# Two pairs of attention units to a visit of the tensor engine: all scores together, all values together

## The chip, the cores and the metric

The kernel runs on one core of one Trainium2 chip. A core has a matrix engine (TensorE, PE in the profile, with its weight loads as PEld), a vector engine (VectorE, DVE), a scalar engine (ScalarE, ACT), a general engine (GpSimd, POOL) and a sync engine (SyncE, SP) that here issues DMAs. Each engine runs its own instructions in the order in which the program lists them, and they wait for each other with semaphores. Matrix products are written to PSUM, which has eight banks; the other data lie in SBUF. The metric is the device time of one execution in microseconds (us).

## The reference

Banded attention over 8 batches, 8 heads, 576 positions and head size 64, followed by a feed-forward layer. Everything is float32.

```python
scores = scale * np.matmul(q, k.transpose(0, 1, 3, 2))
mask = (rel >= 0) & (rel < 64)            # rel = query position - key position
scores = np.where(mask, scores, -1e9)
attn = softmax(scores)                     # exp(s - max), divided by (sum + 1e-9)
x = np.matmul(attn, v)                     # 8*576 = 4608 tokens of 8*64 = 512 columns
h = x @ w_in                               # 512 -> 2048
out = np.maximum(0.01 * h, h) @ w_out      # 2048 -> 512
```

## The kernel before

**Units and pairs.** The attention is cut into 72 units: 64 queries of one batch with all 8 heads. A unit sees 128 keys, its own block of 64 and the one before. Two units make a pair `m` (36 of them), and a pair is one step of the attention. The feed-forward layer is cut into 9 chunks of 512 tokens, four pairs each, and each chunk into 16 steps, one for each block of 128 of the 2048 hidden columns.

**Feed-forward.** In a step, `mm1(c, f)` (line 450) makes one block of h from x with 12 matmuls of 128x128 by 128x512: x and the weights are split into a high and a low part, and three products are summed over four blocks of 128. ScalarE then applies the leaky maximum and casts the result to its high part `gh` (lines 462 and 468), VectorE subtracts to get the low part `gl` (line 472). `mm2` (line 488) multiplies `gh` and `gl` with the second weights into four accumulator banks, `o0` to `o3`, with 12 more matmuls (line 504). `mm2` of a step is issued after `mm1` of the next, so that the scalar and vector work of a step lies beside matmuls. When a chunk is done, `evict` (line 510) copies the four banks out on ScalarE into two buffers and stores them; `flush` calls it.

**Attention of one pair.** From pair 8 on it goes so:

- `scores_2(u)` (line 361): 64 matmuls of 64x64 by 64x64 (line 234, in `quarter_scores`), into two PSUM banks. Scores lie with keys across partitions. It also issues the loads of the next k and q on SyncE's queue.
- `shield_2(u)` (line 370): VectorE scales and masks both halves of the scores out of PSUM (line 380), GpSimd takes the maximum over the partitions of each half (line 388), VectorE subtracts it (line 393) and ScalarE takes the exponential (line 394). The subtraction of the second half is `second_2(u)`, issued a step later.
- `sums_2(u)` (line 401): GpSimd sums each half over the partitions (line 406).
- `values_2(u)` (line 409): 32 matmuls of 128x64 by 128x64 (line 419) into one bank, and the load of the next v.
- `invert_2(u)` (line 426): VectorE adds 1e-9 to both halves of the sums and takes the reciprocal (lines 431 to 433).
- `norm_2(u)` (line 435): VectorE multiplies the values with it (line 440), ScalarE casts the product to the high part of x (line 443), VectorE subtracts to get the low part (line 444). The next chunk's `mm1` reads both.

The probabilities of a pair lie in one buffer, `probs_of`, so the values of a pair have to be taken before the next pair's scores are shielded.

**Order of the work.** There are three parts: a beginning whose order is written out by hand (`ORDER`, line 45), 16 jobs that finish chunks 0 and 1 (line 581), and the last loop over chunks 2 to 8 (lines 606 to 625). In the last loop a pair takes four steps. In the second of the four, between `mm1` and `mm2`, TensorE does the values of a pair and then the scores of the next; this is called a visit below. In the third step come the second subtraction, the norm and the sums. Lines 628 to 637 tie every engine to the program's order.

PSUM's eight banks are the four accumulators `o0` to `o3`, and `o`, `h`, `s`, `t`. `mm1` takes `o` and `h` in turn (`of_h`), values take `s` or `t` (`of_a`), scores one of either set.

Of the kernel before, what the change touches and what calls it, by code (L numbers as in the profile page):

```python
# [13 lines left out]
F32 = mybir.dt.float32  # L14
F32R = mybir.dt.float32r
U32 = mybir.dt.uint32
AF = mybir.ActivationFunctionType
ALU = mybir.AluOpType
# [3 lines left out]
B, H, S, D = 8, 8, 576, 64  # L22
DM, DF = 512, 2048
NT = B * S
P = 128
NP = H // 2
QB = 64
NQB = S // QB
NU = B * NQB
CH = 512  # L30
NCHUNK = NT // CH
UPC = CH // QB
UNITS = 2
TURNED = 2 * UPC
PACE = 12
ROOMS = 3
OWN = 4
# [37 lines left out]
SCALE = 1.0 / math.sqrt(D)  # L75
# [7 lines left out]
def flat(t):  # L83
    return t.rearrange("p a b -> p (a b)") if len(t.shape) == 3 else t


@with_exitstack
def band_attention_ffn(ctx: ExitStack, tc: tile.TileContext, qT, kB, vW, w_in, w_out, eye_mask, out):
    nc = tc.nc
    const = ctx.enter_context(tc.tile_pool(name="const", bufs=1))  # L90
    ld = ctx.enter_context(tc.tile_pool(name="ld", bufs=2))
# [1 line left out]
    wk = ctx.enter_context(tc.tile_pool(name="wk", bufs=2))  # L93
# [4 lines left out]
    def bank(tag, name):  # L98
        return ps_e.tile([P, 512], F32, tag=tag, name=name)


    of_h, of_a = cycle("oh"), cycle("st")
# [21 lines left out]
        return more[:, m - 2] if m in (2, 3) else qs[m % 2]  # L124

    def k_of(m):
        return more[:, m] if m in (2, 3) else ks[m % 2]

    def v_of(m):
        return vs[m % 2 if m < TURNED // 2 else 0]  # L130

    def v_heads(m, w):
        return v_of(m)[:, w, : H * (D + 1)].rearrange("p (h d) -> p h d", h=H)

    def load_q(m):
        if m < NU // 2:
            nc.sync.dma_start(q_of(m), qT[m])

    def load_k(m):
        if m < NU // 2:  # L140
            nc.sync.dma_start(k_of(m), kB[m])

    def load_v(m):
        if m < NU // 2:
            nc.sync.dma_start(v_of(m)[:, :, : H * (D + 1)], vW[m])

    def key_blocks(u):

# [63 lines left out]
    probs = {}  # L212

    def x_of(u):
        c, w = divmod(u, UPC)
        if c not in xs:
            xs[c] = [xp.tile([P, KT, CH], F32R, tag=f"x{i}", name=f"x{i}_{c}") for i in range(2)]
        return [x[:, :, w * QB : (w + UNITS) * QB] for x in xs[c]]
# [5 lines left out]
    def quarter_scores(m, ps, begun, more=False):  # L224

        q = q_of(m)
        for w in range(UNITS):
            k = key_blocks(UNITS * m + w)
            for p in range(NP):
                for i in range(2):  # L230
                    for j in range(2):
                        s, t = slice(64 * j, 64 * j + 64), slice(64 * i, 64 * i + 64)
                        c = (2 * p + w) * QB
                        nc.tensor.matmul(  # L234
                            ps[j][t, c : c + QB], k[i][s, p], q[s, w, p],
                            start=not begun and (not more or (w, p) == (0, 0)),
                            stop=not begun and not more or (w, p) == (UNITS - 1, NP - 1),
                        )

    def mask_of(u):  # L240

        kinds = [v % NQB == 0 for v in (u, u + 1)]
        if any(kinds):
            return away[:, 1:] if kinds[0] else away[:, :2]
        return away[:, :1]
# [115 lines left out]
    def scores_2(u):  # L361
        if u >= NU:
            return
        ps = [bank(next(t), f"s{u}_{j}") for j, t in enumerate((of_a, of_h))]
        quarter_scores(u // 2, ps, False)
        probs[u] = ps
        load_k(u // 2 + 1)
        load_q(u // 2 + 2)

    def shield_2(u):  # L370

        if u >= NU:
            return
        ps = probs.pop(u)
        a = mask_of(u).bitcast(F32)
        n = a.shape[1]
        a = flat(a)[:, None, :].broadcast_to([P, H // n, n * QB])
        for j in range(2):
            e, s = (x.rearrange("a (b c) -> a b c", c=n * QB) for x in (probs_of[:, j], ps[j]))
            nc.vector.scalar_tensor_tensor(e, s, SCALE, a, ALU.mult, ALU.add)  # L380
            if j == 0:
                first_most = most(u, j)
        exps_2(0, first_most)
        probs[u] = most(u, 1)
# [11 lines left out]
    def second_2(u):  # L396

        if u < NU:
            exps_2(1, probs.pop(u))

    def sums_2(u):
        if u >= NU:
            return
        raw = flat(wk.tile([P, 512, 2], U32, tag="raw", bufs=3, name=f"n{u}")).bitcast(F32)
        for j in range(2):
            nc.gpsimd.partition_all_reduce(raw[:, 512 * j : 512 * j + 512], probs_of[:, j], P, ReduceOp.add)  # L406
        probs[u] = raw

    def values_2(u):
        if u >= NU:  # L410
            return
        raw = probs.pop(u)
        v = [v_heads(u // 2, w) for w in range(2)]
        ps = bank(next(of_a), f"o{u}")
        for w in range(2):
            for p in range(NP):
                for j in range(2):
                    c = (2 * p + w) * QB
                    nc.tensor.matmul(  # L419
                        ps[64 * j : 64 * j + 64, c : c + QB], v[w][:, 2 * p + j, :D], probs_of[:, j, c : c + QB],  # L420
                        start=True, stop=True,
                    )
        probs[u, 0] = ps, raw
        load_v(u // 2 + 1)

    def invert_2(u):
        if u >= NU:
            return
        ps, raw = probs[u, 0]
        r, t = raw[:, :512], raw[:, 512:]  # L430
        nc.vector.tensor_scalar_add(r[:64], r[:64], 1e-9)
        nc.vector.tensor_scalar_add(r[64:], t[64:], 1e-9)
        nc.vector.reciprocal(r, r)  # L433

    def norm_2(u):
        if u >= NU:
            return
        ps, raw = probs.pop((u, 0))
        r, t = raw[:, :512], raw[:, 512:]
        nc.vector.tensor_tensor(t, ps, r, ALU.mult)  # L440
        hi, lo = x_of(u)
        t = t.rearrange("a (b c) -> a b c", b=NP)
        nc.scalar.copy(hi, t)  # L443
        nc.vector.tensor_tensor(lo, t, hi.bitcast(F32), ALU.subtract)  # L444

    g = {}

    def mm1(c, f, part):  # L450
# [37 lines left out]
    def mm2(c, f, part):  # L488


        gh, gl = g.pop((c, f, part.start))
        wh, wl = wo[f]
        for i in range(part.start // P, part.stop // P):
            split = c == 1 or c == 0 and i < 2
            begin = f == 0 or split and f == half
            end = f == FT - 1 or split and f == half - 1
            if begin:
                pool, tag = (ps_o, f"o{i}")
                if c == 1 and f == 0 and i > 1:
                    pool, tag = ps_e, "st"[i - 2]  # L500
                acc[c, i] = pool.tile([P, DM], F32, tag=tag, name=f"acc{c}_{i}_{f}")
            ts = slice(i * P, (i + 1) * P)
            for n, (a, b) in enumerate(((gh, wh), (gh, wl), (gl, wh))):
                nc.tensor.matmul(  # L504
                    acc[c, i], a[:, ts], b, start=begin and n == 0, stop=end and n == 2
                )
            if end:
                due.append(partial(evict, c, i, f, split))
# [24 lines left out]
    def flush():  # L533
        while due:
            due.pop(0)()
# [42 lines left out]
    prev = jobs[-1]  # L578
    jobs = [(c, half + k, whole) for c in range(2) for k in range(half)]
    first_late = len(jobs) - UPC - 3  # L580
    for n, job in enumerate(jobs):
        weave(mm1(*job), late[n * PACE : (n + 1) * PACE])
        if first_late <= n < len(jobs) - 1:
            u = TURNED - 2 + (n - first_late) // 2 * 2
            if (n - first_late) % 2 == 0:
                if u >= TURNED:
                    values_2(u)
                scores_2(u + 2)
                shield_2(u + 2)
            else:  # L590
                second_2(u + 2)
                if u >= TURNED:
                    norm_2(u)
                sums_2(u + 2)
        mm2(*prev)
        flush()
        if first_late < n < len(jobs) - 1 and (n - first_late) % 2 == 0:
            invert_2(u)
        if n == 4:
            reload(0)  # L600
        if n == 14:
            reload(1)
        prev = job


    steps = [(c, f) for c in range(2, NCHUNK) for f in range(FT)]
    for n, (c, f) in enumerate(steps):
        u = 3 * UPC + n // 4 * 2
        for step in mm1(c, f, whole):
            step()  # L610
        if n % 4 == 1:
            values_2(u)
            scores_2(u + 2)
            shield_2(u + 2)
        if n % 4 == 2:
            second_2(u + 2)
            norm_2(u)
            sums_2(u + 2)
        mm2(*prev)
        flush()  # L620
        if n % 4 == 1:
            invert_2(u)
        prev = (c, f, whole)
    mm2(*prev)
    flush()


    last = {}
# [53 lines left out]
```

## Time and profile before

| what | value |
| --- | --- |
| median of 3 runs | 905.27 us (904.88 to 905.3) |
| profiled execution | 906.58 us, of which the span from first to last instruction is 904.8 us |
| VectorE busy | 497.2 us (55%) |
| ScalarE busy | 304.9 us (34%) |
| GpSimd busy | 321.2 us (36%) |
| data read and written in DRAM | 56.62 and 11.01 MB, 75 GB/s over the span |

The profile is that of one execution, and its rows are read so. A row of a timeline has the start in us from the first instruction, the duration, the engine, the line of the kernel, the operation, what it writes and reads, its shape, and how many instructions are merged in it. Matmuls overlap, so the distance between two starts says more than a duration. A row of groups ends with the busy time in us, the mean of one in ns, and the idle time of the engine before them with what ended it.

### The profile page before, as it was taken

The page shows a single profiled execution, that of the slowest core. Times are in us where ns is not written, and L with a number is a line of the kernel's source. Part 1 is how long each engine was busy: PE and PEld are TensorE (multiplying, and loading weights), DVE is VectorE, ACT ScalarE, POOL GpSimd, SP SyncE. Part 2 cuts the span into 40 slices and gives each one's busy share as a digit, 9 for nine tenths or more (in the row PEclk, how much of TensorE's full clock was granted, in tenths as well). Part 3 has the DMA queues.
Part 4 walks back from the last instruction along what each step waited for, and adds up shares of the span by engine and source line. Part 5 has one row for each costly group of instructions (what it writes and reads, how often), then busy time and mean ns, then how long its engine had stood idle before and what let it go on. Part 6 is the DMA issues. An engine that isn't in the chain of part 4 may idle for free.

```text
span 904.8 us, 16195 instructions
## 1 busy us (share of the span) xinstructions
PE 896.4 (99%) x7021; PEld 735.6 (81%) x7021; DVE 497.2 (55%) x638; ACT 304.9 (34%) x517; POOL 321.2 (36%) x132
## 2 busy tenths in 40 slices
PE   8999999999999999999999999999999999999998
PEld 5887888888888888888888888888888888888886
DVE  6999892388644545555555545444555555531111
ACT  4665654232222232223322222223222332223222
POOL 4422000577433434444444434333434444400000
PEclk9999999999999999999999999999999999999999
DMA  7753741223311011111211121112101221001001
GB/s 286 254 175 116 245 140 70 71 95 119 118 47 47 27 63 53 48 48 47 95 47 49 47 95 47 49 47 85 40 25 40 72 71 36 25 1 47 0 1 47
DMA packets 31895, 68.68 MB, mean 76 GB/s; under 512 B 3024, under 2 KB 3152, under 8 KB 31824
## 3 DMA queue, kind: packets, MB, share of 16 engines
q1 hardware_dynamic: 27360, 51.95, 16.9%
q10 hardware_dynamic: 4464, 15.70, 5.7%
q8 instruction: 55, 0.90, 0.4%
q14 instruction: 16, 0.13, 0.0%
HBM read 56.62 MB, written 11.01 MB: 75 GB/s over the span
## 4 chain that ended last, share of the span: by engine, by line
PE 93%; DVE 4%; issue 1%; DMA 1%; ACT 1%; POOL 0%; ACTq 0%; DVEq 0%
PE acc L504 42%; PE h L457 41%; PE s L234 4%; PE o L419 3%; PE o L323 1%; DMA room<-eye_mask 1%; PE s L268 1%; DVE gl L472 1%; DVE raw L185 1%; DVE w L202 0%; DVE raw L189 0%; DVE raw L197 0%; DVE wi L209 0%; PE s L302 0%; DVE e L293 0%
## 5 line engine op out<-in xcount | busy, mean ns | idle before, releaser
L457 PE MATMUL h<-x,wi 128*128 128x512 f32 (+1 forms) x1440 | 339.1, 384 | 0.1
L457 PEld LDWEIGHTS h<-x,wi 128*128 128x128 f32 x1440 | 265.7, 188 | 54.7 <-DVE x L444 0.4
L504 PE MATMUL acc<-wo,gh 128*128 128x512 f32 x936 | 293.7, 395 | 0.3 <-DVE s L521 0.3
L472 DVE TENSOR_TENSOR gl<-g,gh 128x512 fp32r<-128x512 f32 (+1 forms) x147 | 100.2, 682 | 325.1 <-ACT gh L468 324.9
L388 POOL PARTITION_ALL_REDUCE mx<-e x56 | 108.2, 1933 | 382.1 <-DVE e L380 359.1
L504 PEld LDWEIGHTS acc<-wo,gh 128*128 128x128 f32 x936 | 172.7, 188 | 37.6 <-DVE s L521 0.5
L406 POOL PARTITION_ALL_REDUCE n<-e x56 | 183.2, 3271 | 38.6 <-ACT e L394 38.6
L462 ACT ACTIVATE g<-h 128x512 f32<-128x512 f32 (+1 forms) x147 | 86.6, 589 | 317.0 <-PE h L457 315.8
L504 PE MATMUL acc<-wo,gl 128*128 128x512 f32 x468 | 182.3, 390 | 0.0
L504 PEld LDWEIGHTS acc<-wo,gl 128*128 128x128 f32 x468 | 87.9, 188 | 19.0
L394 ACT ACTIVATE e<-e 128x512 f32<-128x512 f32 x56 | 35.4, 633 | 200.0 <-DVE e L393 200.0
L433 DVE RECIPROCAL n<-n 128x512 f32<-128x512 f32 x28 | 93.9, 3353 | 1.0
L468 ACT CAST gh<-g 128x512 fp32r<-128x512 f32 (+1 forms) x147 | 89.9, 612 | 9.0 <-PE acc L504 4.0
L457 PE MATMUL h<-x,w 128*128 128x512 f32 x324 | 77.8, 389 | 0.0
L444 DVE TENSOR_TENSOR x<-n,x 128x512 fp32r<-128x512 f32 x28 | 61.7, 2202 | 19.2 <-ACT x L443 19.2
L457 PEld LDWEIGHTS h<-x,w 128*128 128x128 f32 x324 | 60.8, 188 | 12.7
L504 PE MATMUL acc<-w,gh 128*128 128x512 f32 x216 | 66.7, 390 | 0.0
L393 DVE TENSOR_TENSOR e<-e,mx 128x512 f32<-128x512 f32 x56 | 38.4, 686 | 36.9 <-POOL mx L388 36.9
L504 PEld LDWEIGHTS acc<-w,gh 128*128 128x128 f32 x216 | 40.5, 188 | 8.5
L234 PE MATMUL s<-q,k 64*64 64x64 f32 x2160 | 41.0, 226 | 1.1 <-DMA q<-qT 1.1
L504 PE MATMUL acc<-w,gl 128*128 128x512 f32 x108 | 42.0, 389 | 0.0
L234 PEld LDWEIGHTS s<-q,k 64*64 64x64 f32 x2160 | 36.3, 140 | 5.7 <-issue 2.1
(70 smaller groups left out, 508.8 us busy)
## 6 DMA issues: line engine op xcount, KB each, us to landing
v<-vW SPq DMA_DIRECT2D x32, 520.0 KB, 4.7
q<-qT SPq DMA_DIRECT2D x34, 256.0 KB, 4.7
k<-kB SPq DMA_DIRECT2D x33, 256.0 KB, 4.6
raw<-w_out ACTq DMA_DIRECT2D x15, 512.0 KB, 3.7
out<-o SPq DMA_DIRECT2D x30, 256.0 KB, 2.2
raw<-w_in ACTq DMA_DIRECT2D x14, 512.0 KB, 3.8
room<-vW SPq DMA_DIRECT2D x4, 520.0 KB, 5.8
sum<-e SPq DMA_DIRECT2D x6, 256.0 KB, 2.0
```

The lines of the kernel that those rows point to most:

```text
L234: nc.tensor.matmul(ps[j][t, c : c + QB], k[i][s, p], q[s, w, p], start=not begun and (not more or (w, p) == (0, 0)), stop=not begun and no ...
L388: nc.gpsimd.partition_all_reduce(mx, probs_of[:, j], P, ReduceOp.max)
L393: nc.vector.tensor_tensor(e, e, mx, ALU.subtract)
L394: nc.scalar.activation(e, e, AF.Exp)
L406: nc.gpsimd.partition_all_reduce(raw[:, 512 * j : 512 * j + 512], probs_of[:, j], P, ReduceOp.add)
L433: nc.vector.reciprocal(r, r)
L444: nc.vector.tensor_tensor(lo, t, hi.bitcast(F32), ALU.subtract)
L457: nc.tensor.matmul(ps, a[:, k, :], b[:, k, part], start=n == 0, stop=n == len(terms) - 1)
L462: nc.scalar.activation(t[0], ps, AF.Prelu, alpha=0.01)
L468: nc.scalar.copy(g[c, f, part.start][0][:, part], t[0])
L472: nc.vector.tensor_tensor(lo, t[0], hi.bitcast(F32), ALU.subtract)
L504: nc.tensor.matmul(acc[c, i], a[:, ts], b, start=begin and n == 0, stop=end and n == 2)
```

## The change

From pair 12 on (the first pair of the fourth chunk, `PAIRED = 12`), the last loop takes two pairs in eight steps. In step 1 of the eight, after `mm1` of that step and the outstanding `mm2`, come the scores of both pairs, and then at once the `mm2` of step 1. In step 5, between `mm1` and `mm2`, come the values of both pairs. The vector, scalar and GpSimd work is spread over steps 1 to 6. Scores, probabilities, maxima, sums and values of the second pair get buffers of their own out of the three `raw` buffers and the `y` buffer, which are no longer used for weights by then. The second pair's scores go to banks `o` and `h`. The values are loaded without the column of ones (`vL`, 512 columns instead of 520). The loop before the last one no longer does the scores of pair 12.

```diff
+PAIRED = 12
...
     def k_of(m):
+        if m >= PAIRED:
+            return (ks[0], later.get("k"), ks[1])[(m - PAIRED) % 3]
         return more[:, m] if m in (2, 3) else ks[m % 2]
 
     def v_of(m):
-        return vs[m % 2 if m < TURNED // 2 else 0]
+        if m >= PAIRED:
+            return (vs[0], later.get("v"))[m % 2][:, :, : H * D]
+        return vs[m % 2 if m < TURNED // 2 else 0][:, :, : H * (D + 1)]
...
+    later = {}
+
+    def open_room():
+
+        e, n, v = (wk.tile([P, 512, 2], U32, tag="raw", bufs=3, name=f"late_{x}") for x in "env")
+        e, n, v = (flat(x).bitcast(F32).rearrange("p (a b) -> p a b", a=2) for x in (e, n, v))
+        k = flat(wk.tile([P, NP, 2, D], F32, tag="y", bufs=1, name="late_k").rearrange("p a b c -> p a (b c)"))
+        later.update(e=e, n=n, v=v, k=k.rearrange("p (a b c) -> p a b c", a=UNITS, b=NP))
+
+    def e_of(m):
+        return (probs_of, later["e"])[m % 2]
+
+    def scores_3(m):
+        ps = [bank(t, f"s{m}_{j}") for j, t in enumerate((next(of_h), next(of_h)) if m % 2 else "st")]
+        quarter_scores(m, ps, False)
+        probs[m] = ps
+
+    def shield_3(m):
...
+        for j in range(2):
+            e, s = (x.rearrange("a (b c) -> a b c", c=n * QB) for x in (e_of(m)[:, j], ps[j]))
+            nc.vector.scalar_tensor_tensor(e, s, SCALE, a, ALU.mult, ALU.add)
+
+    def spare(name):
+        return wk.tile([P, 512], F32, tag="pT", bufs=1, name=name)
+
+    def most_3(m):
+        for j in range(2):
+            b = 2 * (m % 2) + j
+            mx = later["n"][:, b - 1] if b in (1, 2) else spare(f"mx{m}_{j}")
+            nc.gpsimd.partition_all_reduce(mx, e_of(m)[:, j], P, ReduceOp.max)
+            probs[m, j] = mx
+
+    def exps_3(m):
+        for j in range(2):
+            e = e_of(m)[:, j]
+            nc.vector.tensor_tensor(e, e, probs.pop((m, j)), ALU.subtract)
+            nc.scalar.activation(e, e, AF.Exp)
+
+    def sums_3(m, j):
+        t = probs[m, "sum"] = spare(f"n{m}") if j else later["n"][:, m % 2]
+        nc.gpsimd.partition_all_reduce(t, e_of(m)[:, j], P, ReduceOp.add)
+
+    def fold_3(m):
+        r, t = later["n"][:, m % 2], probs.pop((m, "sum"))
+        nc.vector.tensor_scalar_add(r[64:], t[64:], 1e-9)
+        nc.vector.tensor_scalar_add(r[:64], r[:64], 1e-9)
+        nc.vector.reciprocal(r, r)
+
+    def values_3(m):
+        ps = bank("st"[m % 2], f"o{m}")
...
+    def product_3(m):
+        r = later["n"][:, m % 2]
+        nc.vector.tensor_tensor(r, probs.pop(m), r, ALU.mult)
+        nc.scalar.copy(x_of(UNITS * m)[0], r.rearrange("a (b c) -> a b c", b=NP))
+
+    def low_3(m):
+        hi, lo = x_of(UNITS * m)
+        t = later["n"][:, m % 2].rearrange("a (b c) -> a b c", b=NP)
         nc.vector.tensor_tensor(lo, t, hi.bitcast(F32), ALU.subtract)
...
+            ahead = u + 2 < UNITS * PAIRED
...
+                if ahead:
+                    scores_2(u + 2)
+                    shield_2(u + 2)
             else:
-                second_2(u + 2)
+                if ahead:
+                    second_2(u + 2)
                 if u >= TURNED:
                     norm_2(u)
-                sums_2(u + 2)
+                if ahead:
+                    sums_2(u + 2)
...
+    open_room()
+    load_k(PAIRED + 1)
+    load_v(PAIRED + 1)
     steps = [(c, f) for c in range(2, NCHUNK) for f in range(FT)]
     for n, (c, f) in enumerate(steps):
-        u = 3 * UPC + n // 4 * 2
+        m = PAIRED + n // 8 * 2
+        at = n % 8 if m < NU // 2 else None
         for step in mm1(c, f, whole):
             step()
-        if n % 4 == 1:
-            values_2(u)
-            scores_2(u + 2)
-            shield_2(u + 2)
-        if n % 4 == 2:
-            second_2(u + 2)
-            norm_2(u)
-            sums_2(u + 2)
+        if at == 2:
+            exps_3(m + 1)
+            sums_3(m, 0)
+            sums_3(m, 1)
+            sums_3(m + 1, 0)
+        if at == 4:
+            fold_3(m)
+            sums_3(m + 1, 1)
+        if at == 5:
+            for x in (m, m + 1):
+                values_3(x)
+                load_v(x + 2)
+            product_3(m)
+            fold_3(m + 1)
+            low_3(m)
+        if at == 6:
+            product_3(m + 1)
+            low_3(m + 1)
+        if prev:
+            mm2(*prev)
+            flush()
+        prev = (c, f, whole)
+        if at == 1:
+            for x in (m, m + 1):
+                scores_3(x)
+                load_q(x + 2)
+            load_k(m + 2)
+            load_k(m + 3)
+            shield_3(m)
+            shield_3(m + 1)
+            most_3(m)
+            exps_3(m)
+            most_3(m + 1)
+            mm2(*prev)
+            flush()
+            prev = None
+    if prev:
         mm2(*prev)
         flush()
-        if n % 4 == 1:
-            invert_2(u)
-        prev = (c, f, whole)
-    mm2(*prev)
-    flush()
...
+    vL = vW[PAIRED:].reshape(-1, P, 2, H, D + 1)[..., :D].reshape(-1, P, 2, H * D)
```

More of the change, by code (lines that the diff above doesn't have):

```diff
@@ L87, in band_attention_ffn @@
 @with_exitstack
-def band_attention_ffn(ctx: ExitStack, tc: tile.TileContext, qT, kB, vW, w_in, w_out, eye_mask, out):
+def band_attention_ffn(ctx: ExitStack, tc: tile.TileContext, qT, kB, vW, vL, w_in, w_out, eye_mask, out):
     nc = tc.nc
@@ L126, in k_of @@
     def k_of(m):
+        if m >= PAIRED:
+            return (ks[0], later.get("k"), ks[1])[(m - PAIRED) % 3]
         return more[:, m] if m in (2, 3) else ks[m % 2]
     def v_of(m):
-        return vs[m % 2 if m < TURNED // 2 else 0]
+        if m >= PAIRED:
+            return (vs[0], later.get("v"))[m % 2][:, :, : H * D]
+        return vs[m % 2 if m < TURNED // 2 else 0][:, :, : H * (D + 1)]
     def v_heads(m, w):
-        return v_of(m)[:, w, : H * (D + 1)].rearrange("p (h d) -> p h d", h=H)
+        return v_of(m)[:, w].rearrange("p (h d) -> p h d", h=H)
     def load_q(m):
@@ L144, in load_v @@
         if m < NU // 2:
-            nc.sync.dma_start(v_of(m)[:, :, : H * (D + 1)], vW[m])
+            nc.sync.dma_start(v_of(m), vL[m - PAIRED] if m >= PAIRED else vW[m])
     def key_blocks(u):
@@ new lines, in e_of @@
+    def e_of(m):
[5 more added lines that the diff above has]
+    def shield_3(m):
+        ps = probs.pop(m)
+        a = mask_of(UNITS * m).bitcast(F32)
+        n = a.shape[1]
+        a = flat(a)[:, None, :].broadcast_to([P, H // n, n * QB])
+        for j in range(2):
+            e, s = (x.rearrange("a (b c) -> a b c", c=n * QB) for x in (e_of(m)[:, j], ps[j]))
+            nc.vector.scalar_tensor_tensor(e, s, SCALE, a, ALU.mult, ALU.add)
@@ new lines, in sums_3 @@
+    def sums_3(m, j):
[8 more added lines that the diff above has]
+        ps = bank("st"[m % 2], f"o{m}")
+        for w in range(UNITS):
+            v = v_heads(m, w)
+            for p in range(NP):
+                for j in range(2):
+                    c = (2 * p + w) * QB
+                    nc.tensor.matmul(
+                        ps[64 * j : 64 * j + 64, c : c + QB], v[:, 2 * p + j], e_of(m)[:, j, c : c + QB],
+                        start=True, stop=True,
+                    )
+        probs[m] = ps
@@ L448, in band_attention_ffn @@
+    def product_3(m):
[5 more added lines that the diff above has]
+        t = later["n"][:, m % 2].rearrange("a (b c) -> a b c", b=NP)
+        nc.vector.tensor_tensor(lo, t, hi.bitcast(F32), ALU.subtract)
     g = {}
@@ L603, in band_attention_ffn @@
         prev = job
+    open_room()
+    load_k(PAIRED + 1)
+    load_v(PAIRED + 1)
     steps = [(c, f) for c in range(2, NCHUNK) for f in range(FT)]
     for n, (c, f) in enumerate(steps):
-        u = 3 * UPC + n // 4 * 2
+        m = PAIRED + n // 8 * 2
+        at = n % 8 if m < NU // 2 else None
         for step in mm1(c, f, whole):
             step()
-        if n % 4 == 1:
-            values_2(u)
-            scores_2(u + 2)
-            shield_2(u + 2)
-        if n % 4 == 2:
-            second_2(u + 2)
-            norm_2(u)
-            sums_2(u + 2)
+        if at == 2:
[35 more added lines that the diff above has]
+    if prev:
         mm2(*prev)
         flush()
-        if n % 4 == 1:
-            invert_2(u)
-        prev = (c, f, whole)
-    mm2(*prev)
-    flush()
     last = {}
@@ L668 @@
     eye_mask = np.concatenate([eye, mask[:QB].transpose(2, 1, 0).reshape(P, 3 * QB), -eye], axis=1)
-    feeds = {"qT": qT, "kB": kB, "vW": vW, "w_in": wi, "w_out": wo, "eye_mask": eye_mask}
+    feeds = {"qT": qT, "kB": kB, "vW": vW, "vL": vL, "w_in": wi, "w_out": wo, "eye_mask": eye_mask}
     feeds = {n: np.ascontiguousarray(a) for n, a in feeds.items()}
```

## The prediction

> **What bounds the kernel now.** I read the page from the top: busy shares, granted clock, chain that ended last.
>
> ```profile
> PE 896.4 (99%) x7021; PEld 735.6 (81%) x7021; DVE 497.2 (55%) x638; ACT 304.9 (34%) x517; POOL 321.2 (36%) x132
> ...
> PEclk9999999999999999999999999999999999999999
> ...
> PE 93%; DVE 4%; issue 1%; DMA 1%; ACT 1%; POOL 0%; ACTq 0%; DVEq 0%
> ```
>
> TensorE (PE) is busy 99% of the span, always in the top class of granted clock, and is 93% of the chain. Only what changes PE's own stream, or makes it wait, can move the time. So next comes the timeline of PE alone, in the part that the change rewrites.
>
> ```profile
> 333.61 2.88 PE L457 MATMUL h<-x,wi 128*128 128x512 f32 x12
> 336.42 1.15 PE L419 MATMUL o<-e,v 128*64 128x64 f32 x32
> 337.50 1.16 PE L234 MATMUL s<-q,k 64*64 64x64 f32 x64
> 338.59 0.74 PE L504 MATMUL acc<-wo,gh 128*128 128x512 f32 x2
> ...
> 341.49 2.88 PE L457 MATMUL h<-x,wi 128*128 128x512 f32 x12
> 344.21 0.61 PE L504 MATMUL acc<-wo,gh 128*128 128x512 f32 x2
> ...
> 346.93 2.88 PE L457 MATMUL h<-x,wi 128*128 128x512 f32 x12
> ...
> 357.81 2.88 PE L457 MATMUL h<-x,wi 128*128 128x512 f32 x12
> ```
>
> A step without attention lasts 346.93 − 341.49 = 5.44 us: 2.72 for `mm1`, 2.72 for `mm2`, 0.227 a matmul. The step with a visit lasts 341.49 − 333.61 = 7.88, so a visit of one pair's values and the next pair's scores costs 2.44. It recurs every 24.20 us (333.61 to 357.81), which is 4 × 5.44 + 2.44: nothing else waits. Two places in the trace have a visit of one kind alone, first scores, then values.
>
> ```profile
> 159.74 2.88 PE L457 MATMUL h<-x,w 128*128 128x512 f32 x12
> 162.55 1.16 PE L234 MATMUL s<-q,k 64*64 64x64 f32 x64
> 163.64 0.73 PE L504 MATMUL acc<-wo,gh 128*128 128x512 f32 x2
> ...
> 166.50 2.88 PE L457 MATMUL h<-x,w 128*128 128x512 f32 x12
> ```
> ```profile
> 793.40 2.88 PE L457 MATMUL h<-x,w 128*128 128x512 f32 x12
> 796.22 1.15 PE L419 MATMUL o<-e,v 128*64 128x64 f32 x32
> 797.30 0.73 PE L504 MATMUL acc<-wo,gh 128*128 128x512 f32 x2
> ...
> 800.16 2.88 PE L457 MATMUL h<-x,w 128*128 128x512 f32 x12
> ```
>
> Both last 6.76, so scores alone cost 1.32 and values alone 1.32. Together in one visit they cost 2.44, not 2.64. Call c the work of one kind for one pair and w the price of one change of matmul shape (128x128, 128x64, 64x64). Alone is c + 2w, together 2c + 3w. So w = 2.64 − 2.44 = 0.20 and c = 0.92, each good to about 0.02 as the rows are rounded.
>
> **The sum.** Before, two pairs (8 steps) take two joined visits: 4.88, six changes of shape. After, they take one visit of two pairs' scores and one of two pairs' values, four changes: 2 × (2 × 0.92 + 2 × 0.20) = 4.48. That is 0.40 less a group.
>
> The count: values of pairs 12 to 35 are visited in the last loop, 23 times with the next scores, once alone (the visit at 796.22). After, twelve groups. The scores of pair 12 also leave the visit of job 13 in the loop before, which then holds values alone.
>
> ```profile
> 212.25 2.88 PE L457 MATMUL h<-x,w 128*128 128x512 f32 x12
> ...
> 220.21 1.07 PE L457 MATMUL h<-x,w 128*128 128x512 f32 x4
> ...
> 231.09 3.16 PE L457 MATMUL h<-x,wi 128*128 128x512 f32 x12
> 234.09 0.62 PE L504 MATMUL acc<-w,gh 128*128 128x512 f32 x2
> ```
> ```profile
> 229.11 2.26 DVE L444 TENSOR_TENSOR x<-n,x 128x512 fp32r<-128x512 f32 x1 [0.69 <-ACT x L443]
> ```
>
> That visit costs 7.96 − 5.44 = 2.52. Before: 23 × 2.44 + 1.32 + 2.52 = 59.96. After: 12 × 4.48 + 1.32 = 55.08. Gain 4.88.
>
> The second pair of rows is `mm1` at the start of the third chunk: 3.00 instead of 2.72. Its second matmul reads the low part of x, which VectorE (DVE) finishes at 229.11 + 2.26 = 231.37. After the change, `second_2(24)` no longer stands ahead of that work. By the durations below x is ready near 227.8, while PE, 1.20 earlier, needs it near 230.1. So 0.28 goes as well.
>
> Against it stands the way back to large matmuls. `mm2` after a joined visit takes 341.49 − 338.59 = 2.90, after a single kind 2.86 (166.50 − 163.64, 800.16 − 797.30), undisturbed 2.72. Whether the longer visits behave like the long or the short ones no row shows: 0 to 24 × 0.04 = 0.96 lost. I take half, 0.5.
>
> Could the second pair in a visit pay something of its own? It has other operands and other PSUM banks (`o`/`h` after `s`/`t`). The bounds: from below 0, or a gain of 0.02 by the rounding of c; from above 2w = 0.40, as if it were a visit by itself. I take 0, because one pair's scores already alternate between two banks, matmul by matmul, and 64 of them pass in 1.09 us. The Trainium skill (TensorEngine Tiling (Array Packing), Tiling Modes, Key Properties) says that changing the tiling mode, not just the tile, drains TensorE. By that rule a second pair in the same mode pays 0 and the sum stays; no run here shows two pairs in a row.
>
> Net: 4.88 + 0.28 − 0.5 = 4.66.
>
> **What lies beside PE, and whether it still fits.** Each engine runs in program order, so I lay one group out by hand, with these durations:
>
> ```profile
> L433 DVE RECIPROCAL n<-n 128x512 f32<-128x512 f32 x24 | 80.5, 3353 | 0.8
> L472 DVE TENSOR_TENSOR gl<-g,gh 128x512 fp32r<-128x512 f32 x93 | 62.5, 673 | 212.4 <-ACT gh L468 212.4
> L444 DVE TENSOR_TENSOR x<-n,x 128x512 fp32r<-128x512 f32 x23 | 51.9, 2258 | 15.8 <-ACT x L443 15.8
> L393 DVE TENSOR_TENSOR e<-e,mx 128x512 f32<-128x512 f32 x46 | 31.6, 686 | 30.2 <-POOL mx L388 30.2
> L380 DVE SCALAR_TENSOR_TENSOR e<-s,away 128x512 f32<-128x512 f32 x46 | 29.6, 685 | 5.1 <-PE s L234 5.1
> L432 DVE TENSOR_SCALAR n<-n 64x512 f32<-64x512 f32 x24 | 27.4, 1140 | 0.4
> L440 DVE TENSOR_TENSOR n<-o,n 128x512 f32<-128x512 f32 x23 | 15.7, 683 | 0.0
> L431 DVE TENSOR_SCALAR n<-n 64x512 f32<-64x512 f32 x24 | 9.9, 411 | 0.0
> ```
> ```profile
> L406 POOL PARTITION_ALL_REDUCE n<-e x46 | 150.5, 3271 | 32.1 <-ACT e L394 32.1
> L388 POOL PARTITION_ALL_REDUCE mx<-e x46 | 89.2, 1938 | 286.3 <-DVE e L380 267.5 <-DVE e L393 18.8
> ```
> ```profile
> 337.47 0.59 ACT L530 COPY o<-acc 128x512 f32<-128x512 f32 x1 [1.87 <-DMA out<-o]
> 337.95 0.60 ACT L462 ACTIVATE g<-h 128x512 f32<-128x512 f32 x1
> 338.58 0.62 ACT L468 CAST gh<-g 128x512 fp32r<-128x512 f32 x1
> ```
>
> Let 0 be the start of `mm1` in step 1. PE: `mm2` of step 0 from 2.72, scores from 5.44, `mm2` of step 1 ends at 10.40; then `mm1` of steps 2 and 3 in a row, `mm2(2)` from 15.84; `mm1(5)` ends at 26.72, the two values by 28.96; the next group's `mm1(8)` starts at 42.56 and its first low part of x is due at 42.8.
>
> DVE shields four halves from 6.6 to 9.3. GpSimd (POOL) runs four maxima from 7.3 to about 15.1, then four sums, 3.27 each, to about 28.2. DVE's second subtraction of the first pair waits for POOL until about 11.3, with the low part of step 2 queued behind; that is not needed before 15.0 (`mm1(2)` ends at 13.12, plus 0.60, 0.62, 0.67), and `mm2(2)` reads it at 16.3. Margin 1.3.
>
> The end of the group is the tight place. DVE: `fold_3(m)` 23.3 to 28.2 (1.14 + 0.41 + 3.35), low part of step 5 to 28.9, `product_3(m)` to 29.6, `fold_3(m+1)` to 34.5, `low_3(m)` to 36.8, low part of step 6 to 37.5, `product_3(m+1)` to 38.2, the cast to 38.8, `low_3(m+1)` to 41.1. Due 42.8: margin 1.7, at the six starts of chunks 3 to 8.
>
> The chunk's start moves too: `mm2` of step 0 now follows `mm1(1)` at once, without the visit between. It needs the accumulator banks that ScalarE (ACT) copies out; the last copy ends at 337.47 + 0.59 = 338.06, which is 4.45 after 333.61, and the fourth bank is due at 2.72 + 9 × 0.227 = 4.76. Margin 0.3, price if gone: the delay, six times.
>
> On SyncE's queue the loads of q, k and v now come in two bursts a group, and wait there for the visit that frees their buffers. Behind them stand only the output stores of a chunk's end, steps later, and each load has about 48 us. Cost 0; were a load late, its own visit would show it.
>
> **The rivals.** *A: small waits on PE.* The visit of job 13 costs 0.08 more than the regular one. If every one of the 24 new visits pays that, 1.9 of the gain goes: 902.5. A POOL chain one reduction (3.27) late would do less: `fold_3(m+1)` would start at 31.5, 1.9 later, and x come 0.2 late, six times, 1.2 lost, or 901.9. For it: several tiles are new, and each may need a wait. Against it: every producer has a margin above. Chance 0.16.
>
> *B, slower: it is the pair that pays, not the change of shape.* If the 0.20 on either side belongs to each pair's fresh operands and banks, a second pair pays up to 0.40: a group costs 4 × 1.32 = 5.28, the total is 12 × 5.28 + 1.32 − 59.96 = +4.72, less 0.28: 909.7. The place is between the two pairs of a visit; it decides from 4.66 / 24 = 0.19 a visit. For it: no row has two pairs in a row. Against it: the joined visit, where values and scores also have different tiles and banks, pays only one 0.20 between them. Chance 0.08, and 0.04 for part of it that leaves no change.
>
> *C: PE's instruction supply.* A visit of 128 short matmuls is longer than any now (96 in 338.59 − 336.42 = 2.17 us). If the second 64 scores came at the values' pace, 1.08 / 32 = 34 ns, instead of 17, each scores visit would lose 1.09, in all 13.1: 913.7. The Trainium skill (TensorE: Matmul & The Clock Gate, Step-by-step: what each phase is for) gives about 62 ns a matmul for decoding in software. By that figure, as an estimate, the second 64 scores would take 4.0 us and the time would be 935. The trace speaks against that: 96 matmuls in 2.17 us are 23 ns each, changes of shape included. Chance 0.04.
>
> **How the numbers follow.** The profiled execution took 906.58 us (span 904.8), the runs' median 905.27. The gain lies wholly inside the span, so it is taken from the median: 905.27 − 4.66 = 900.6, forecast 900.7, chance 0.72, its own range 899.9 to 902. The range: below, no loss on the way back, w at 0.22 and 0.2 for the runs' spread; above, rival A's 902.5 and half of its 1.2. That is 899.9 to 903.2. B and C are left out. A measurement of this kernel can tell about 0.2% from no change, 1.8 us. Faster by more: the forecast and nearly all of A, 0.86. Within: 0.06 (part of B, the end of A). Slower: 0.08 (the rest of B, and C).
>
> **What would show it.** Right: in PE's timeline one block of 128 matmuls of line 234's form lasting 1.9 to 2.0 us between two `mm2`, one of 64 values matmuls of the same length, steps with a visit of 7.6 to 7.8 and all others at 5.44, a period near 48.0 for eight steps (now 48.4), and 3.00 back at 2.72. For A: gaps before the first matmul of a visit, or an `mm1` at a chunk's start over 2.72. For B: a pause in the middle of a block. For C: the second half of a scores block slower than the first. The prediction is wrong if a step without a visit exceeds 5.44 anywhere in the last loop, or if a visit of two pairs costs more than 2.4.

## The result and the profile after

The changed kernel takes 916.47 us (median of 4 runs, 916.27 to 917.15) against 905.28 (median of 4 runs of the kernel before): 1.0122 times as long, 95% interval 1.011 to 1.0134. That is 11.2 us slower; 4.6 faster was forecast, and the time lies far outside the range.

The page of the changed kernel, the same parts as before:

```profile
PE 894.1 (98%) x7021; PEld 731.6 (80%) x7021; DVE 501.5 (55%) x638; ACT 304.7 (33%) x517; POOL 315.4 (34%) x132
...
PEclk9999999999999999999999999999999999999999
...
PE 79%; DVE 13%; ACT 3%; POOL 3%; issue 1%; DMA 1%; ACTq 0%; DVEq 0%
```

TensorE does no more work than before, but it has fallen from 93% to 79% of the chain that ended last, and VectorE has risen from 4% to 13%. So PE waits for VectorE somewhere. Who waited for whom, on PE, longest first:

```profile
PE acc L586 <- DVE gl L554: 12.5, 12, 1.0
```

Twelve waits, one for each group of two pairs, all of a second matmul (`mm2`, line 586 now) for the low part `gl` (line 554 now). The timeline of PE through one group shows where:

```profile
286.04 0.61 PE L586 MATMUL acc<-wo,gh 128*128 128x512 f32 x2
...
288.85 0.27 PE L239 MATMUL s<-q,late_k 64*64 64x64 f32 x2
...
290.87 0.73 PE L586 MATMUL acc<-wo,gh 128*128 128x512 f32 x2
...
293.73 5.60 PE L539 MATMUL h<-x,wi 128*128 128x512 f32 x24
299.17 0.61 PE L586 MATMUL acc<-wo,gh 128*128 128x512 f32 x2
300.83 0.50 PE L586 MATMUL acc<-wo,gl 128*128 128x512 f32 x1 [1.04 <-DVE gl L554]
...
303.24 2.88 PE L539 MATMUL h<-x,wi 128*128 128x512 f32 x12
...
308.68 2.88 PE L539 MATMUL h<-x,w 128*128 128x512 f32 x12
311.50 1.15 PE L512 MATMUL o<-e,v 128*64 128x64 f32 x32
312.48 1.10 PE L512 MATMUL o<-late_e,late_v 128*64 128x64 f32 x32
313.51 0.73 PE L586 MATMUL acc<-wo,gh 128*128 128x512 f32 x2
...
316.36 2.88 PE L539 MATMUL h<-x,w 128*128 128x512 f32 x12
```

Read it in three steps. The visits do what was forecast. Scores: from `mm2(0)` at 286.04 to `mm1(2)` at 293.73 are 7.69 us, 2.25 more than two undisturbed blocks of 2.72. Values: 316.36 − 308.68 − 5.44 = 2.24. Together 4.49, forecast 4.48 without the way back. Then `mm2(2)`, which starts at 299.17 and ends when `mm1(4)` begins at 303.24: 4.07 instead of 2.72. Its third matmul, the first to read `gl`, starts 1.2 late, and the matmuls after it make up the rest of 1.35. Twelve times 1.35 is 16.2 us.

Why `gl` is late is in the timelines of VectorE and GpSimd at that place:

```profile
298.00 2.78 DVE L554 TENSOR_TENSOR gl<-g,gh 128x512 fp32r<-128x512 f32 x1 [1.96 <-ACT gh L550]
300.70 0.68 DVE L492 TENSOR_TENSOR late_e<-late_e,late_n 128x512 f32<-128x512 f32 x1
...
303.81 1.12 DVE L554 TENSOR_TENSOR gl<-g,gh 128x512 fp32r<-128x512 f32 x1 [1.84 <-ACT gh L550]
```
```profile
297.90 3.31 POOL L497 PARTITION_ALL_REDUCE late_n<-e  x1
302.14 3.23 POOL L497 PARTITION_ALL_REDUCE n<-e  x1 [0.93 <-ACT late_e L493]
```

The subtraction started in time, at 298.00, and took 2.78 us where it takes 0.69 elsewhere. GpSimd had begun the first sum of the group at 297.90, 0.1 earlier. It is the first sum, and not another, because the four maxima end just then and the first half's exponentials are long done. The subtraction of the next step, at 303.81, starts 1.67 into the second sum and takes 1.12, but nobody waits for it.

### The profile page after: what moved, and what is told of

It is laid out like the page before. It is cut to its first block, busy times and chain, and to the rows that moved or that the text cites. A ratio compares the mean times of both kernels' runs of the same rounds, so it can differ in the third digit from the quotient of the medians.

```text
span 914.6 us, 16196 instructions
## 1 busy us (share of the span) xinstructions
PE 894.1 (98%) x7021; PEld 731.6 (80%) x7021; DVE 501.5 (55%) x638; ACT 304.7 (33%) x517; POOL 315.4 (34%) x132
## 3 DMA queue, kind: packets, MB, share of 16 engines
q1 hardware_dynamic: 25824, 51.75, 16.3%
## 4 chain that ended last, share of the span: by engine, by line
PE 79%; DVE 13%; ACT 3%; POOL 3%; issue 1%; DMA 1%; ACTq 0%; DVEq 0%
PE acc L586 38%; PE h L539 34%; DVE gl L554 4%; PE o L512 3%; POOL late_n L486 2%; PE s L239 2%; DVE e L492 2%; DVE e L477 2%; DVE late_e L477 2%; ACT e L493 1%; ACT gh L550 1%; ACT g L544 1%; PE o L328 1%; DVE raw L202 1%; DMA room<-eye_mask 1%
## 5 line engine op out<-in xcount | busy, mean ns | idle before, releaser
L554 DVE TENSOR_TENSOR gl<-g,gh 128x512 fp32r<-128x512 f32 (+1 forms) x147 | 132.5, 902 | 350.0 <-ACT gh L550 349.8
L486 POOL PARTITION_ALL_REDUCE mx<-e x12 | 21.4, 1782 | 331.1 <-DVE e L477 331.1
L503 DVE RECIPROCAL late_n<-late_n 128x512 f32<-128x512 f32 x24 | 80.5, 3353 | 0.8
L393 POOL PARTITION_ALL_REDUCE mx<-e x8 | 15.2, 1900 | 94.1 <-DVE e L385 90.8
L493 ACT ACTIVATE e<-e 128x512 f32<-128x512 f32 x24 | 15.2, 632 | 95.2 <-DVE e L492 95.2
L497 POOL PARTITION_ALL_REDUCE n<-e x12 | 38.8, 3234 | 11.1 <-ACT late_e L493 11.1
L497 POOL PARTITION_ALL_REDUCE n<-late_e x12 | 40.5, 3377 | 5.3 <-DVE late_n L501 5.3
L497 POOL PARTITION_ALL_REDUCE late_n<-e x12 | 39.8, 3313 | 0.0
L497 POOL PARTITION_ALL_REDUCE late_n<-late_e x12 | 39.7, 3311 | 0.0
```

The costliest lines, as they stand in the source:

```text
L486: nc.gpsimd.partition_all_reduce(mx, e_of(m)[:, j], P, ReduceOp.max)
L493: nc.scalar.activation(e, e, AF.Exp)
L497: nc.gpsimd.partition_all_reduce(t, e_of(m)[:, j], P, ReduceOp.add)
L554: nc.vector.tensor_tensor(lo, t[0], hi.bitcast(F32), ALU.subtract)
```

## The experiments

The theory: a VectorE operation with two operands in SBUF that starts while GpSimd reduces is held until the reduction is nearly done. The rivals: the four loads of a group, which go out some 5 to 8 us earlier, slow it; or ScalarE is late, since two exponentials stand before the activation of step 2. A wider form of the theory: GpSimd slows whatever VectorE does.

### The first sum behind the low part

```diff
-            mx = later["n"][:, b - 1] if b in (1, 2) else spare(f"mx{m}_{j}")
+            mx = later["n"][:, 2 - b] if b in (1, 2) else spare(f"mx{m}_{j}")
```

> Two of the maxima exchange their buffers, so that GpSimd's first sum of a group overwrites a buffer that VectorE reads only after the low part of step 2. Theory (a subtraction of two SBUF tensors that starts beside a GpSimd reduction is held until that is nearly done): the low part of step 2 takes 0.69 us instead of 2.78, mm2 of step 2 takes 2.72 instead of 4.07, all twelve waits (16.2 us) go, and the time is 916.5 - 16.2 = 900.3 us. Rival 1 (the burst of four loads that lands there slows it): the loads stay where they are, so 2.78 and 916.5. Rival 2 (ScalarE is late because two exponentials stand before the activation of step 2): nothing changes, 916.5.

Measured: 900.31 us (5 runs, 900.14 to 900.42), the kernel before 905.26 on the same chip, ratio 0.9944, interval 0.993 to 0.9957. VectorE, GpSimd and PE in this kernel:

```profile
296.85 0.69 DVE L554 TENSOR_TENSOR gl<-g,gh 128x512 fp32r<-128x512 f32 x1 [1.96 <-ACT gh L550]
```
```profile
298.31 3.53 POOL L497 PARTITION_ALL_REDUCE late_n<-e  x1 [1.46 <-DVE late_e L492]
```
```profile
298.02 0.62 PE L586 MATMUL acc<-wo,gh 128*128 128x512 f32 x2
...
300.74 2.88 PE L539 MATMUL h<-x,wi 128*128 128x512 f32 x12
```

The sum now waits for VectorE and starts after the subtraction, which takes 0.69; `mm2(2)` is back at 2.72. The subtraction still starts 1.5 us after `mm1(2)`'s end, behind the same exponential (1.96 us of idle time before it, as before), so ScalarE's lateness was not it; in the step before, with ScalarE free, the subtraction of the changed kernel starts 1.48 after its `mm1`. The loads stayed too. The whole loss was this one coincidence (916.47 − 900.31 = 16.16), and the kernel without it is faster than both.

### The same subtraction with one operand in PSUM

```diff
-            t.append(wk.tile([P, CH], F32, tag="g", bufs=1, name=f"g{c}_{f}_{part.start}")[:, part])
+            t.append(ps if c > 1 else wk.tile([P, CH], F32, tag="g", bufs=1, name=f"g{c}_{f}_{part.start}")[:, part])
```

> From chunk 2 on the activation is written back into its PSUM bank, so the low part is PSUM minus SBUF; the GpSimd sum starts where it did. Theory (it is the second SBUF operand that is held): 0.7 us beside the sum, the waits go, about 900.3 us. Rival 1 (loads) and a wider rival (any VectorE work is slow beside a GpSimd sum): 2.78 us stays, 916.5. If ScalarE or VectorE is slower out of PSUM, up to a few tenths a step, hidden under 2.72 us of matmuls.

Measured: 900.28 us (4 runs, 900.19 to 900.44), ratio 0.9944, interval 0.9931 to 0.9958. VectorE and GpSimd:

```profile
296.55 0.69 DVE L554 TENSOR_TENSOR gl<-h,gh 128x512 fp32r<-128x512 f32 x1 [1.85 <-ACT gh L550]
297.16 2.29 DVE L492 TENSOR_TENSOR late_e<-late_e,late_n 128x512 f32<-128x512 f32 x1
...
301.85 0.69 DVE L554 TENSOR_TENSOR gl<-h,gh 128x512 fp32r<-128x512 f32 x1 [1.80 <-ACT gh L550]
```
```profile
296.58 3.31 POOL L497 PARTITION_ALL_REDUCE late_n<-e  x1
300.22 3.24 POOL L497 PARTITION_ALL_REDUCE n<-e  x1 [0.33 <-ACT late_e L493]
```

The subtraction is not held. The next operation of VectorE, which has both operands in SBUF and starts 0.58 into the sum, is held in its place: 2.29 us instead of the 0.68 it took in the changed kernel, where it ran after the hold. The wider form falls.

The first row alone does not show that the operand is the reason: here the subtraction begins 0.03 before the sum, and in the changed kernel it began 0.10 after it, so the order of the two starts differs as well. The subtraction of the next step parts the two. It begins 1.63 into the second sum, where the one in the changed kernel began 1.67 into it, and takes 0.69 instead of 1.12. So the second SBUF operand makes the difference; a later run shows the same from 0.51 into a sum.

### Loads elsewhere

```diff
             sums_3(m + 1, 1)
+            load_q(m + 2)
+            load_q(m + 3)
+            load_k(m + 2)
+            load_k(m + 3)
...
-                load_q(x + 2)
-            load_k(m + 2)
-            load_k(m + 3)
```

> The four loads of a group are issued in step 4 instead of step 1, so that none lands beside the low part of step 2. Theory: no change, 2.78 us and 916.5 us. Rival 1 (the loads slow it): 0.69 us and about 900 us.

Measured: 917.05 us, a single run. SyncE's queue in this kernel shows that the edit did not do what it was for:

```profile
290.72 2.29 SPq L142 DMA_DIRECT2D q<-qT  x2
...
293.54 0.42 SPq L146 DMA_DIRECT2D k<-kB  x1
```

The loads still go out between 290.7 and 294. The first leaves 1.25 us after the first matmul of the scores, as in the changed kernel. The program's order ties an instruction only to those of its own engine; on SyncE nothing stood between, so the loads left when their buffers came free, as before. The run says nothing of the loads. What excludes them are the two runs above, in which they stayed and the subtraction took 0.69. By an estimate they had also landed by then: in the changed kernel the last one goes out at 292.51, the median from issue to landing of these loads is 3.3 to 3.5 us, and the subtraction starts at 298.00.

### A shorter reduction

```diff
-        nc.gpsimd.partition_all_reduce(t, e_of(m)[:, j], P, ReduceOp.add)
+        op = ReduceOp.add if m % 2 or j else ReduceOp.max
+        nc.gpsimd.partition_all_reduce(t, e_of(m)[:, j], P, op)
```

> The first sum of each group is a maximum instead (the probabilities of that half are then divided by another number), which takes 1.9 us instead of 3.3. Theory: the low part of step 2 is let go 1.66 us after the reduction's start instead of 2.79, takes about 1.6 us instead of 2.78, and the wait in mm2 of step 2 falls from 1.35 to between 0 and 0.3 us: 900.3 to 904 us. Rivals 1 and 2: 2.78 us and 916.5 us.

Measured: 902.2 us, a single run. VectorE, GpSimd and PE:

```profile
296.99 1.57 DVE L555 TENSOR_TENSOR gl<-g,gh 128x512 fp32r<-128x512 f32 x1 [1.96 <-ACT gh L551]
```
```profile
296.90 1.86 POOL L498 PARTITION_ALL_REDUCE late_n<-e  x1
```
```profile
298.62 0.49 PE L587 MATMUL acc<-wo,gl 128*128 128x512 f32 x1
298.95 0.62 PE L587 MATMUL acc<-wo,gh 128*128 128x512 f32 x2
```

The hold follows the reduction's length: it ends 296.99 + 1.57 − 296.90 = 1.66 us after the start of a maximum, 300.78 − 297.90 = 2.88 after that of a sum. PE still slips by a tenth (0.33 from one matmul to the next, instead of 0.23). Over the twelve groups `mm2(2)` takes 2.84 to 2.89 instead of 2.72, that is 0.12 to 0.17 a group or 1.4 to 2.0 us in all, and this single run is 1.9 us above the kernel without the coincidence.

### What a change of matmul shape costs

Two runs on the kernel with the exchanged buffers part the visits again, with the same instructions.

```diff
+        if at == 1:
+            scores_3(m)
+            load_q(m + 2)
...
-            for x in (m, m + 1):
-                scores_3(x)
-                load_q(x + 2)
+            scores_3(m + 1)
+            load_q(m + 3)
```

> On the kernel with the exchanged buffers (900.3 us): the scores of the first pair of a group move one mm2 ahead, so that the two pairs' scores are two visits instead of one; the same instructions, two more changes of matmul shape in each of twelve groups. Theory (a change of shape costs 0.19 to 0.20 us): + 12 x 2 x 0.195 = 4.7, 905.0 us. Rival B of the prediction (each pair pays by itself, joined or not): 900.3 us.

The second run does the same, and to the values as well:

```diff
         if at == 5:
-            for x in (m, m + 1):
-                values_3(x)
-                load_v(x + 2)
+            values_3(m)
+            load_v(m + 2)
+            mm2(*prev)
+            flush()
+            prev = None
+            values_3(m + 1)
+            load_v(m + 3)
```

> As the run before, and the two values visits of a group are also parted by one mm2: four more changes of shape in a group. Theory: + 12 x 4 x 0.195 = 9.4, 909.7 us, 4.7 more than with the scores alone parted. Rival B: 900.3 us.

Measured, with the kernel before at 905.79 on the same chip: scores apart 905.72 (10 runs, ratio 1.0, interval 0.999 to 1.0009), both apart 909.75 (4 runs, ratio 1.0046, interval 1.0029 to 1.0062). Against before: joined −4.95, scores apart −0.07, both apart +3.96. Two changes of shape in twelve groups cost 4.88, two more 4.03, that is 0.20 and 0.17 each; the intervals, 0.8 to 1.5 us either way on the three times, do not part these two. The parted values in PE's timeline:

```profile
307.88 2.88 PE L539 MATMUL h<-x,w 128*128 128x512 f32 x12
310.69 1.15 PE L512 MATMUL o<-e,v 128*64 128x64 f32 x32
311.77 0.73 PE L586 MATMUL acc<-wo,gh 128*128 128x512 f32 x2
...
314.72 1.15 PE L512 MATMUL o<-late_e,late_v 128*64 128x64 f32 x32
315.80 3.02 PE L539 MATMUL h<-x,w 128*128 128x512 f32 x12
318.65 0.62 PE L586 MATMUL acc<-w,gh 128*128 128x512 f32 x2
```

From 307.88 to 318.65 are 10.77, less three blocks of 2.72: 2.61, where the joined values cost 2.24. The difference of 0.37 is two changes. So it is the change of shape that costs time and not the pair.

### The row of before that was misread

The prediction took the subtraction behind the low part of x (line 444, 2.26 us) as that operation's own price. In this run, on the kernel before, its first operand is moved to PSUM.

```diff
-        nc.vector.tensor_tensor(t, ps, r, ALU.mult)
+        nc.vector.tensor_tensor(ps, ps, r, ALU.mult)
         hi, lo = x_of(u)
-        t = t.rearrange("a (b c) -> a b c", b=NP)
+        t = ps.rearrange("a (b c) -> a b c", b=NP)
```

> On the kernel before: the product of values and reciprocal stays in its PSUM bank, so the subtraction that gives the low part of x has one SBUF operand instead of two, beside the same GpSimd sum. Theory (two SBUF operands are held beside a reduction): that subtraction takes 0.69 us instead of 2.26; it is off the path, so the time stays within 0.3 us of 905.3, and only the first mm1 of chunk 2 falls from 3.00 to 2.72. Rival (2.26 us is what this operation costs by itself, as the prediction took it): 2.26 stays.

Measured: 905.54 us, a single run, against 905.79. The group of that line, one of its rows with the sum beside it, then the first `mm1` of chunk 2:

```profile
L444 DVE TENSOR_TENSOR x<-o,x 128x512 fp32r<-128x512 f32 x23 | 15.9, 692 | 15.0 <-ACT x L443 15.0
```
```profile
349.30 0.69 DVE L444 TENSOR_TENSOR x<-o,x 128x512 fp32r<-128x512 f32 x1 [0.65 <-ACT x L443]
```
```profile
348.79 3.23 POOL L406 PARTITION_ALL_REDUCE n<-e  x1 [1.39 <-ACT e L394]
```
```profile
230.30 2.88 PE L457 MATMUL h<-x,wi 128*128 128x512 f32 x12
233.02 0.62 PE L504 MATMUL acc<-w,gh 128*128 128x512 f32 x2
```

0.69 for each of the 23, and 2.72 for the `mm1`. They start 0.50 or 0.51 into a sum, where the same operation with two SBUF operands started 0.53 into it and took 2.26. The 2.26 was a hold all along, in a place where only the first `mm1` of chunk 2 waited for it. The trace of before had shown it. Of its rows for this operation, one beside a sum and the last of all, when GpSimd had no work left:

```profile
350.46 2.26 DVE L444 TENSOR_TENSOR x<-n,x 128x512 fp32r<-128x512 f32 x1 [0.69 <-ACT x L443]
```
```profile
349.93 3.23 POOL L406 PARTITION_ALL_REDUCE n<-e  x1 [1.39 <-ACT e L394]
```
```profile
806.34 0.69 DVE L444 TENSOR_TENSOR x<-n,x 128x512 fp32r<-128x512 f32 x1 [0.69 <-ACT x L443]
```

The Trainium skill states the rule (SBUF — State Buffer, Who interferes with whom): a VectorE instruction with two SBUF inputs contends with a GpSimd instruction that reads SBUF, since its second input comes through the read interface that they share; the contention is an exclusive lock, and the order of issue decides who is blocked. These traces agree for the operand: about 0.5 us into a sum, 2.26 us with two in SBUF and 0.69 with one in PSUM. They differ a little on the end, as the hold ends 0.43 us before the sum's recorded end (300.78 against 297.90 + 3.31 = 301.21), on an engine whose recorded spans are rough.

## Why the prediction was wrong

**The step that failed** is in the part on what lies beside PE: the low part of step 2 ready at 15.0, because `mm1(2)` ends at 13.12 "plus 0.60, 0.62, 0.67", read at 16.3, "Margin 1.3". The 0.67 is the mean of 93 rows of line 472 in the kernel before. 46 of them start during a sum, but none less than 2.71 us into it, when the hold is all but over, and they take 0.63 to 0.68 us; the others start beside no reduction. One row outside those 93 starts earlier, 0.97 into the sum that begins at 169.79, and shows what the mean hid:

```profile
170.76 1.89 DVE L472 TENSOR_TENSOR gl<-g,gh 128x512 fp32r<-128x512 f32 x1 [2.83 <-ACT gh L468]
```

The change put the subtraction 0.1 us behind the start of a sum, twelve times, and there it takes 2.78: `gl` was ready at 17.5 on the prediction's clock (whose 0 is 283.32 in this trace), not at 15.0. The layout by hand did have GpSimd's sums from about 15.1 and the subtraction just before 15.0; it held the two engines to be independent. In the trace the sum starts at 14.6, because the maxima follow each other at 1.69 to 1.77 us and not at the 1.94 of the layout. The subtraction starts at 14.7 and not at 14.3, as it begins 1.55 after the end of `mm1(2)` where the layout counted 1.22. So the sum was first. That the two met within 0.1 us in every group is an accident of this layout; that a sum can hold the subtraction is not.

**Point by point.** For the two places ahead of the groups and for `low_3`, rows of the changed kernel's timeline of PE and its groups of VectorE:

```profile
210.81 2.88 PE L539 MATMUL h<-x,w 128*128 128x512 f32 x12
...
217.65 0.62 PE L539 MATMUL h<-x,w 128*128 128x512 f32 x2
```
```profile
228.53 2.88 PE L539 MATMUL h<-x,wi 128*128 128x512 f32 x12
...
231.25 0.62 PE L586 MATMUL acc<-w,gh 128*128 128x512 f32 x2
```
```profile
L526 DVE TENSOR_TENSOR x<-late_n,x 128x512 fp32r<-128x512 f32 x24 | 15.8, 660 | 8.2 <-ACT x L521 8.2
```

- The sum of the visits held: 4.49 a group against 4.48, and −4.95 in all once the hold is gone, against −4.66.
- The loss on the way back was taken at 0.5. It was 0: `mm2` after the visits takes 2.86 (293.73 − 290.87) and 2.85 (316.36 − 313.51), like the short visits.
- The 0.28 at the start of chunk 2 went, as forecast: that `mm1` takes 231.25 − 228.53 = 2.72 in the changed kernel.
- The visit of job 13 with values alone costs 217.65 − 210.81 − 5.44 = 1.40, not 1.32.
- `low_3` was priced at 2.26 and takes 0.66 on the mean, as GpSimd has no work at that moment. The 1.14 of line 432 in `fold_3` was such a mean too: 27 of its 28 rows start beside a maximum and take 1.17, and the last, with no reduction beside it, takes 0.42, which is also the mean in the changed kernel. The margin at the chunks' starts was wider than laid out. The same misreading made these prices too high and that of the low part too low.
- The accumulators were in time: the steps at the chunks' starts are as long as the others.
- Rival A named small waits and held that every producer had its margin; the wait came at a producer with a margin and was not small. Rivals B (909.7) and C (913.7) lay on the right side and C near the measured time, but neither was what happened: the scores visit has no pause in its middle, and its 128 matmuls and the change of shape take 290.87 − 288.85 = 2.02 us, 16 ns each. The 62 ns that the Trainium skill gives for decoding in software (TensorE: Matmul & The Clock Gate, Step-by-step: what each phase is for) are not paid here. The rule of the Trainium skill that a change of tiling mode, and not of the tile alone, drains TensorE (TensorEngine Tiling (Array Packing), Tiling Modes) agrees with the joined visits, 4.49 against the 4.48 that counts no change within them, and with the 0.37 that parting the values costs; the drain itself is in no row.
- The low end of the range, 899.9, leaves out one of its own terms: w at 0.22 is 24 × 0.02 = 0.48 more, so it comes to 899.4. The measured time lies far on the other side.

So the account closes. Visits: 12 × 4.49 + 1.40 = 55.28 against 59.96 before, −4.68; the start of chunk 2, −0.28; twelve holds, +16.2. That is +11.2, and +11.2 was measured.

## What to carry to other kernels

When a change moves work in time, price each operation beside its new neighbours, and before taking a mean, look at the shortest and longest instance of the same shape: two durations three times apart for one operation are a sign that another engine decides. Here that neighbour is a GpSimd reduction and the victim a VectorE operation with two SBUF operands; put one operand in PSUM, or order the reduction behind the operation by a buffer that it has to wait for. Joining short matmuls of one shape into one visit was worth 0.17 to 0.20 us here for each change of shape saved, and it showed once the hold was gone: 900.3 against 905.3.

## What the hardware showed beyond that

An operation with one SBUF operand can be held as well. In the kernel with the exchanged buffers, the addition of 1e-9 to half the sums (line 501) begins beside a sum, which starts at 304.96, and takes 2.35 us. Beside no reduction it takes 0.42. The reciprocal that follows takes 3.35 in every place, beside a sum or not:

```profile
305.67 2.35 DVE L501 TENSOR_SCALAR late_n<-n 64x512 f32<-64x512 f32 x1
...
309.04 3.35 DVE L503 RECIPROCAL late_n<-late_n 128x512 f32<-128x512 f32 x1
...
313.56 0.42 DVE L501 TENSOR_SCALAR late_n<-n 64x512 f32<-64x512 f32 x1
```

No run tested which property of that addition makes it wait.
